# Memory softmax of a two-layer memory transformer: bias and sum inside the exponent

## The chip, the cores and the metric

The kernel runs on one core of one Trainium2 chip. The metric is device time in microseconds (us) of one execution, given as the median of several runs. The engines are named as the profile names them: PE is TensorE (matmuls and transpositions), PEld its weight loads, DVE is VectorE, ACT is ScalarE, POOL is GpSimd, and SP is SyncE, which issues DMAs.

## What is computed

Two layers, each of which is a recurrent attention with memory followed by a gated feed-forward network, are applied twice with the same weights. The sequence has 2048 tokens of 448 features. The attention goes through it in 64 segments of 32 tokens; each segment sees 8 memory rows and its own 32 tokens (40 keys), with 16 heads of 256 features, and leaves 8 new memory rows for the next segment.

```python
def _A_ref(x, mem0, Wq, Wk, Wv, Wo, seg_len):
    scale = Dh ** (-0.5)
    L = M + seg_len
    idx = jnp.arange(L)
    mask = (idx[:, None] < M) | (idx[:, None] >= idx[None, :])
    mem = mem0
    for s in range(n_seg):
        xs = x[:, s * seg_len:(s + 1) * seg_len, :].copy()
        h = jnp.concatenate([mem, xs], axis=1)
        q, k, v = (jnp.einsum('btd,dhe->bhte', h, W) for W in (Wq, Wk, Wv))
        scores = jnp.einsum('bhqe,bhke->bhqk', q, k) * scale
        scores = jnp.where(mask[None, None], scores, -1000000000.0)
        p = _softmax(scores, axis=-1)
        o = jnp.einsum('bhqk,bhke->bhqe', p, v)
        o = jnp.einsum('bhte,hed->btd', o, Wo)
        mem = o[:, :M, :].copy()
        outs.append(o[:, M:, :])

def _B_ref(x, W_gate, W_up, W_down):
    gate = x @ W_gate
    return (gate * (gate > 0) * (x @ W_up)) @ W_down

x = x + _A_ref(_layernorm(x), ...)
x = x + _B_ref(_layernorm(x), ...)
x = x + _A_ref(_layernorm(x), ...)
x = x + _B_ref(_layernorm(x), ...)
```

The three weights of the query and key side, and of the value and output side, can be multiplied together beforehand: with A = Wq Wk^T for each head, a score is h A h^T times the scale.

## The kernel before

**Stages.** A first stage (about the first 70 us) loads the weights, transposes them on PE and fuses them: `fuse_qk_parts` makes A (tiles `A_sb`, `A3`, `A3z`) and `fuse_vo` makes B = Wv Wo (`B_sb`). It goes through the 16 heads as 8 pairs p. Each pair's products stand in PSUM tiles `aps` and `mxw`, and `evac` moves them to SBUF: a plain copy on ACT (line 94) or on DVE (line 96).

**Steps.** Then `step(g, ff)` runs for g from 0 to 68. The attention of the first layer (chain 0) works on segment g, that of the second layer (chain 1) on segment g - 4; both chains share each step's instructions, with the keys of chain 0 and chain 1 side by side (2 x 40 columns). For g from 4 to 63 both chains are there; the four steps at either end have one. Odd steps also carry the feed-forward work of a block of two segments (`Feed`, argument `ff`); even steps do not.

**Order.** The order of all PE instructions is fixed by hand: `mm` and `tr` chain every matmul to the one before it (`in_order`). DVE, ACT and POOL each run their instructions in one queue, but a planner at build time chooses the order of that queue from when it expects each instruction to be ready; only instructions marked with `keep_in_program_order` are bound to the order of the code. PSUM tiles come from one pool of seven banks (tag `ps`) and one more bank.

**One step around the change.** Heads are worked in two halves, hf = 0 and 1. `open_banks` and `close_bank` make the projected queries (PSUM tile `prj`, 80 columns per matmul), which ACT or DVE casts into `TQ` and `TZ`. For half 1 the four banks are called c0, c2, c1, c3: c0, c2 and c3 are cast by ACT, c1 by DVE. Three kinds of scores are made: `scores_m(hf)` for the memory rows of both chains (PSUM tile `Sm`, 128 x 2 x 40: one partition for a head and a memory row of a chain, two blocks of 40 keys, of which the row needs only its own chain's), and `scores_x(hf)` for the token rows (`Sx`, 128 x 4 x 40). Each goes through a softmax: `weights_begin` (maximum, subtraction, exponent) and `weights_end` (sum, reciprocal, division). For the memory rows the reciprocal is multiplied by `blk`, a 128 x 2 tile of zeros and ones, which clears the block of the other chain. The results are `PM[hf]` and `PX[hf]`.

`flipped` (or `flipped_rows`) then transposes PM or PX on PE into PSUM (`pps`, `ppr`), and DVE copies it to `PT`. `weigh_m` or `weigh_m_rows` multiplies the keys `hk` with PT (PSUM tiles `ya`, `yb`, `ym`), `weigh_x` does so for the token rows (`y1`, `y2`, `y` in the profile), and copies on DVE and ACT (lines 94, 96, 661, 666) bring the results into the tiles Y and Z, which `project_out` and `project_tail` multiply with B (`ox`, `o`).

The order of PE in an even step with both chains, from the memory scores on: Sm of half 0; banks c0, c2, c1, c3 of half 1; the transposition of PM[0]; Sx of half 0; `ya` and `yb`; Sm and Sx of half 1; 69 matmuls of `project_out`; the transpositions of PM[1] and PX[0]; five more tiles of `project_out`; `ym` and `y`. In an odd step the feed's transposition stands ahead of Sm of half 1, and `project_out` of ten tiles and five rounds `gate_up` ahead of `ym`, with PM[1] and PX[0] transposed together (`ppr`) after three of these rounds.

Of the kernel before, what the change touches and what calls it, by code (L numbers as in the profile page):

```python
# [9 lines left out]
F32 = mybir.dt.float32  # L10
I32 = mybir.dt.int32
AF = mybir.ActivationFunctionType
ALU = mybir.AluOpType
AX = mybir.AxisListType
# [4 lines left out]
DH = 256  # L19
MEM = 8  # L20
SEG = 32
L = MEM + SEG
F = 1792
FT = 14
SCALE = DH ** -0.5
MASKVAL = -1.0e6
EPS = 1e-5
LAG = 4
BLK = 2
# [11 lines left out]
ROWS = (slice(0, 64), slice(64, 128))  # L41
# [12 lines left out]
def build_kernel(ctx, tc, A_x, A_mem0, A_Wq, A_Wk, A_Wv, A_Wo, B_W_gate, B_W_up, B_W_down, out,  # L54
                 ntiles=16, nseg=64):
    nc = tc.nc
    P = nc.NUM_PARTITIONS
# [23 lines left out]
    def mm(*a, **k):  # L81
        in_order(nc.tensor.matmul(*a, **k))  # L82
# [9 lines left out]
    def evac(eng, dst, src):  # L92
        if eng is nc.scalar:
            nc.scalar.copy(dst, src)  # L94
        else:
            eng.tensor_copy(dst, src)  # L96


    xa = [glob.tile([P, DM], BF, name=f"xa{i}") for i in range(3)]
    xp = [glob.tile([P, DM], BF, name=f"xp{i}") for i in range(2)]  # L100

    def block(i):
        return slice(TB * i, TB * i + TB)
# [11 lines left out]
                            op0=ALU.arith_shift_right, op1=ALU.bitwise_and)  # L115
    nc.vector.tensor_scalar(out=rowi[:, 2:3], in0=rowi[:, 0:1], scalar1=15, scalar2=None,
                            op0=ALU.bitwise_and)
# [9 lines left out]
    for b in range(4):  # L127
        o = 0 if b % 2 == 0 else MEM
        nc.vector.tensor_scalar(out=maskS[:, b, o:o + SEG], in0=keyf[:, b // 2, :], scalar1=rowf[:, 2:3],
                                scalar2=MASKVAL, op0=ALU.is_gt, op1=ALU.mult)  # L130

    blk = glob.tile([P, 2], F32, name="blk")
    nc.gpsimd.tensor_copy(blk[:, 1:2], rowf[:, 1:2])
    nc.gpsimd.tensor_scalar(out=blk[:, 0:1], in0=blk[:, 1:2], scalar1=-1.0, scalar2=1.0,
                            op0=ALU.mult, op1=ALU.add)
# [4 lines left out]
    A_sb = glob.tile([P, 3, 2, NT, 128], BF, name="A_sb")  # L140
    A3 = glob.tile([P, 2, 12, 128], BF, name="A3")
    A3z = glob.tile([P, 4, 128], BF, name="A3z")
# [71 lines left out]
    with tc.tile_pool(name="pre", bufs=3) as pre:  # L214
# [41 lines left out]
        def dims(t, r, e, c, n=1):  # L256
            o = 64 * c if r == 0 else DM + 64 * ((c + 1) % NPASS)
            return t[:, e, o:o + 64 * n]

        def halves(dst, lhs, rhs):  # L260
            for t in range(2):
                for eo in range(2):
                    mm(dst[ROWS[eo]], lhs(eo, 2 * eo + t), rhs(2 * eo + t), start=(t == 0), stop=(t == 1),
                       tile_position=(0, 64 * eo))

        def fuse_qk_parts(p, qk):
            hf, p4 = divmod(p, 4)
            mx_ps = psum.tile([P, 4, 128], F32, tag="ps", name="mxw")
            for n, (kd, eo) in enumerate([(kd, eo) for eo in range(2) for kd in range(3)] if p < 2 else
                                         [(kd, eo) for kd in range(3) for eo in range(2)]):  # L270
                if n == 3:
                    yield
                aps = psum.tile([P, 3, 128], F32, tag="ps", name="aps")
                for t in range(2):
                    e = 2 * eo + t
                    mm(aps[:, :, :], qk[:, e, kd * 128:kd * 128 + 128], dims(qk, 1, e, 0, 6),
                       start=(t == 0), stop=(t == 1))
                for t in range(2):
                    e = 2 * eo + t
                    mm(mx_ps[:, kd, eo * 64:eo * 64 + 64], qk[:, e, kd * 128:kd * 128 + 128], dims(qk, 1, e, 6),  # L280
                       start=(t == 0), stop=(t == 1))
                evac(nc.scalar if eo or kd == 2 else nc.vector,
                     A_sb[:, kd, hf, eo * 4 + p4:eo * 4 + p4 + 17:8, :], aps[:])
            aps = psum.tile([P, 3, 128], F32, tag="ps", name="aps")
            halves(aps, lambda eo, e: qk[:, e, 384:448], lambda e: dims(qk, 1, e, 0, 6))
            for eo in range(2):
                for t in range(2):
                    e = 2 * eo + t
                    mm(mx_ps[ROWS[hf], 3, eo * 64:eo * 64 + 64], qk[:, e, 384:448], dims(qk, 1, e, 6),
                       start=(t == 0), stop=(t == 1), tile_position=(0, 64 * hf))  # L290
            evac(nc.scalar, A3[:, hf, p4:p4 + 9:4, :], aps[:])
            evac(nc.vector, A_sb[:, 0:3, hf, 24 + p4, :], mx_ps[:, 0:3])
            evac(nc.scalar, A3z[ROWS[hf], p4, :], mx_ps[ROWS[hf], 3])

        def fuse_vo(p, vv, wo):
            hf, p4 = divmod(p, 4)
# [75 lines left out]
    main = ctx.enter_context(tc.tile_pool(name="main", bufs=1))  # L372
# [21 lines left out]
    TZ, PX, PM = [], [], []  # L394
# [97 lines left out]
    def moving(hb, j, idx, chains, rows=slice(0, P)):  # L492

        if len(chains) == 2:
            return hb[rows, j, idx * HI:(idx + 1) * HI].rearrange("p (c k) -> p c k", k=64)[:, :, 0:L]
        c = chains[0]
        return hb[rows, j, idx * HI + 64 * c:idx * HI + 64 * c + L]
# [61 lines left out]
    def queries(hf, g, kd):  # L559
        return TQ[hf][:, g, 2 * kd:2 * kd + 2, :] if kd < 3 else TZ[hf][:, g, :]  # L560

    def weights_of(*a):
        weights_end(*weights_begin(*a))

    def weights_begin(Sp, n, dst, keep, tag):

        mx = main.tile([P, n], F32, tag=f"mx{tag}", name="mx")
        nc.vector.tensor_reduce(mx[:], Sp[:], axis=AX.X, op=ALU.max)
        se = main.tile([P, n, L], F32, tag=f"se{tag}", name="se")
        nc.vector.tensor_tensor(se[:], Sp[:], mx[:].unsqueeze(2).to_broadcast([P, n, L]), op=ALU.subtract)  # L570
        nc.scalar.activation(se[:], se[:], AF.Exp, scale=SCALE)  # L571
        return se, n, dst, keep, tag

    def weights_end(se, n, dst, keep, tag):

        ssum = main.tile([P, n], F32, tag=f"ssum{tag}", name="ssum")
        nc.vector.tensor_reduce(ssum[:], se[:], axis=AX.X, op=ALU.add)  # L577
        rs = main.tile([P, n], F32, tag=f"rs{tag}", name="rs")
        nc.vector.reciprocal(rs[:], ssum[:])
        if keep is not None:  # L580
            nc.vector.tensor_tensor(rs[:], rs[:], keep, op=ALU.mult)
        nc.vector.tensor_tensor(dst[:, :, 0:L], se[:], rs[:].unsqueeze(2).to_broadcast([P, n, L]), op=ALU.mult)

    def flipped(src, n, tag):
# [25 lines left out]
    def step(g, ff):  # L610
# [21 lines left out]
        def scores_m(hf):  # L632
            if not ms:
                return
            Sp = psum.tile([P, 2, L], F32, tag="ps", name="Sm")
            for kd in range(4):
                mm(Sp[:, :, :], queries(hf, 2, kd), moving(hb, j, kd + kd // 3, (0, 1)), start=(kd == 0), stop=(kd == 3))
            weights_of(Sp, 2, PM[hf], blk[:], f"m{hf}")

        def scores_x(hf):  # L640
            Sp = psum.tile([P, 4, L], F32, tag="ps", name="Sx")
            if len(chains) == 1:
                mm(Sp[:, :, :], ident[:], maskS[:], start=True, stop=False, skip_group_check=True)
            for half in range(2):
                for c in chains:
                    for kd in range(4):
                        mm(Sp[:, 2 * half + c, :], queries(hf, 3 * c + half, kd), moving(hb, j, kd + kd // 3, (c,)),
                           start=(len(chains) == 2 and half == c == kd == 0),
                           stop=(half == 1 and c == chains[-1] and kd == 3), skip_group_check=True)
            return Sp  # L650

        def probs_x(hf, Sp):
            weights_of(Sp, 4, PX[hf], None, f"x{hf}")

        def weigh_m(hf, hk, PT):
            if not ms:
# [97 lines left out]
        def feed(*us):  # L754
            if ff is not None:
                for u in us:
                    ff.gate_up(u)
# [36 lines left out]
        if len(chains) == 2:  # L794
# [6 lines left out]
            Sx1 = scores_x(1)  # L801
            probs_x(0, Sx0)
        else:
# [4 lines left out]
            Sx1 = scores_x(1)  # L808
# [4 lines left out]
            load_some()  # L813
        if ff is not None:
            project_out(0, 0, 10)
            half1 = weights_begin(Sx1, 4, PX[1], None, "x1")
            feed(0, 1, 2)
            pt = flipped_rows([(PM[1], 1), (PX[0], 2)])
            feed(3, 4)
            weigh_m_rows(1, hk, pt)  # L820
            feed(5, 6)
            weigh_x(0, hk, pt[:, 128:384])
            weights_end(*half1)
            project_tail()
            ff.down()
            project_out(0, 10, NT)
            project_out(1, 0, 14)
            px1 = flipped(PX[1], 2, "x1")
            ff.norm2()
            project_out(1, 14, 24)  # L830
            ff.feed_on()
            ff.leave()
            project_out(1, 24, NT)
            finish()
            weigh_x(1, hk, px1)
            return
        project_out(0, 0, 23)
        probs_x(1, Sx1)
        pm = flipped(PM[1], 1, "m1")
        px0 = flipped(PX[0], 2, "x0")  # L840
# [88 lines left out]
```

## Time and profile before

| | |
|---|---|
| runs | 1578.43, 1579.52, 1586.14 us; median 1579.52 us |
| the profiled execution | 1585.95 us, its span from first to last instruction 1584.0 us |
| mean granted clock of TensorE | 0.990 |
| one pair of steps in the steady part (814.45 to 858.90 us) | 44.45 us: PE 44.45, PEld 41.55, DVE 32.10, ACT 22.37, POOL 4.56 us busy |
| DVE on the memory softmax (134 times; mean ns) | maximum 236, subtraction 235, sum 234, reciprocal 160, product with blk 157, division 232 |
| ACT on the memory softmax (134 times) | exponent 266 ns |

How to read it: the page's first part gives each engine's busy time, its share of the span and its number of instructions; the second part divides the span into 40 slices and gives the busy share of each in tenths. A line of the timeline has its start and duration in us, the engine, the line of the kernel, the operation, what it writes and reads, and how many instructions it stands for; in square brackets is how long the engine stood idle before it and what ended that. A line of the waits says which engine and line waited for which, with the total in us, how often, and the longest. In the table of groups by form the numbers are total busy us, mean ns of one, and the idle time ahead of them. Copies and casts are recorded on the line of their helper (94 and 96), so they are told apart by their tiles.

### The profile page before, as it was taken

How to read it: one execution, taken by the hardware profiler on the slowest of the kernel's cores; microseconds unless marked ns; L12 is line 12 of the kernel's file. 1: busy time of each engine (PE TensorE's matmuls, PEld its weight loads, DVE VectorE, ACT ScalarE, POOL GpSimd, SP SyncE). 2: the span in 40 equal slices, each digit the busy share in tenths (PEclk: the TensorE clock that was granted, in tenths of full speed). 3: DMA queues.
4: the chain of work that ended last, by engine and by line, in shares of the span. 5: the costliest groups of instructions: out<-in, count | busy, mean ns of one | idle time of the engine just before them, and what ended most of it. 6: DMA issues, size and time to landing. Idle time of an engine off the chain costs nothing.

```text
span 1584.0 us, 98180 instructions
## 1 busy us (share of the span) xinstructions
PE 1552.8 (98%) x45116; PEld 1426.0 (90%) x45116; DVE 1112.6 (70%) x3825; ACT 783.1 (49%) x2307; POOL 174.9 (11%) x308
## 2 busy tenths in 40 slices
PE   9889999999999999999999999999999999999997
PEld 7588899999999999999999999999999999999885
DVE  6755677776777777776777677777767777777663
ACT  6634445544455545554455545544445545544442
POOL 3201110111011111111011111011001111011110
PEclk9989999999999999999999999999999999999998
DMA  9530000000000000000000000000000000000000
GB/s 284 148 80 8 9 10 5 9 10 10 10 10 10 10 10 6 8 10 10 10 10 10 10 10 7 7 10 10 10 10 10 10 10 8 6 8 7 7 7 6
DMA packets 29469, 33.13 MB, mean 21 GB/s; under 512 B 3320, under 2 KB 28160, under 8 KB 29056
## 3 DMA queue, kind: packets, MB, share of 16 engines
q1 hardware_dynamic: 28848, 26.74, 6.2%
q8 instruction: 353, 5.78, 1.5%
q14 instruction: 60, 0.49, 0.1%
q10 hardware_dynamic: 144, 0.11, 0.1%
q0 software_dynamic: 64, 0.01, 0.0%
HBM read 23.18 MB, written 1.84 MB: 16 GB/s over the span
## 4 chain that ended last, share of the span: by engine, by line
PE 95%; DVE 2%; issue 1%; ACT 1%; DMA 1%; POOL 1%; SPq 0%; POOLq 0%; ACTq 0%; DVEq 0%
PE prj L82 30%; PE ox L82 25%; PE ups L82 10%; PE dps L82 6%; PE o L82 5%; PE y L82 4%; PE Sx L82 3%; PE Sm L82 2%; PE aps L82 1%; PE pps L85 1%; PE gps L82 1%; PE bps L82 1%; PE tps L85 1%; PE kps L85 1%; PE ym L82 1%
## 5 line engine op out<-in xcount | busy, mean ns | idle before, releaser
L82 PEld LDWEIGHTS <-B_sb 128*128 128x128 bf16 (+1 forms) x15456 | 495.1, 103 | 29.6 <-issue 21.6
L82 PE MATMUL prj<-hT,A_sb 128*128 128x80 bf16 (+1 forms) x11424 | 430.7, 200 | 0.1
L82 PEld LDWEIGHTS <-A_sb 128*128 128x128 bf16 x11424 | 406.3, 100 | 8.5 <-issue 0.2
L82 PE MATMUL ox<-Y,B_sb 128*128 128x80 bf16 (+4 forms) x5880 | 223.1, 199 | 1.9 <-DVE Y L661 1.9
L94 ACT CAST TQ<-prj 128x480 bf16<-128x480 f32 (+1 forms) x380 | 183.1, 494 | 83.7 <-PE prj L82 59.2
L82 PE MATMUL ox<-Z,B_sb 128*128 128x80 bf16 (+2 forms) x5712 | 217.6, 199 | 1.3 <-DVE Z L661 1.3
L82 PE MATMUL ups<-xT,Wgu_sb 64*128 64x128 bf16 (+1 forms) x3332 | 191.3, 214 | 1.3 <-DVE hh L458 0.8
L82 PE MATMUL gps<-xT,Wgu_sb 64*128 64x128 bf16 (+1 forms) x3332 | 191.3, 214 | 0.4 <-ACT xT L444 0.3
L82 PEld LDWEIGHTS <-Wgu_sb 64*128 64x128 bf16 x6664 | 179.7, 95 | 4.4 <-issue 2.3
L96 DVE CAST TQ<-prj 128x480 bf16<-128x480 f32 (+1 forms) x228 | 129.5, 574 | 17.3 <-PE prj L82 11.7
L458 DVE SCALAR_TENSOR_TENSOR hh<-gps,ut 128x256 bf16<-128x256 f32 (+1 forms) x238 | 94.5, 407 | 48.2 <-ACT ut L457 35.4
L457 ACT CAST ut<-ups 128x256 bf16<-128x256 f32 (+1 forms) x238 | 85.5, 359 | 82.7 <-PE gps L82 64.1
L94 ACT CAST Y<-y 64x128 bf16<-64x128 f32 (+2 forms) x256 | 89.4, 379 | 46.5 <-DVE Y L96 41.5
L96 DVE CAST Y<-y 64x128 bf16<-64x128 f32 (+2 forms) x256 | 102.2, 420 | 14.2 <-ACT Y L94 4.3
L94 ACT COPY hT<-tps 128x256 bf16<-128x256 bf16 x32 | 11.9, 372 | 199.0 <-DVE hT L96 199.0
L96 DVE CAST Z<-y 64x128 bf16<-64x128 f32 (+2 forms) x256 | 99.2, 418 | 12.4 <-ACT Z L94 5.5
L589 DVE COPY PT<-pps 128x128 bf16<-128x128 bf16 (+1 forms) x206 | 49.9, 256 | 80.5 <-PE pps L85 77.7
L94 ACT CAST Z<-y 64x128 bf16<-64x128 f32 (+2 forms) x256 | 89.2, 378 | 23.8 <-DVE Z L96 17.4
L82 PE MATMUL dps<-Wd_sb,hh 128*128 128x448 bf16 x476 | 99.3, 362 | 0.0
L94 ACT CAST TZ<-prj 64x320 bf16<-64x320 f32 (+2 forms) x152 | 56.1, 380 | 86.4 <-DVE TZ L96 78.5
L577 DVE TENSOR_REDUCE ssum<-se 128x2 f32<-128x80 f32 (+1 forms) x270 | 70.8, 274 | 35.8 <-ACT se L571 33.6
L82 PE MATMUL prj<-hT,A 64*128 64x80 bf16 (+1 forms) x3264 | 93.9, 196 | 1.8 <-issue 1.4
(130 smaller groups left out, 2265.7 us busy)
## 6 DMA issues: line engine op xcount, KB each, us to landing
wo<-in_A_Wo_dram SPq DMA_DIRECT2D x8, 448.0 KB, 5.1
nat<-in_A_Wq_dram SPq DMA_DIRECT2D x8, 384.0 KB, 6.1
nat<-in_A_Wk_dram SPq DMA_DIRECT2D x8, 384.0 KB, 6.2
nat<-in_A_Wv_dram SPq DMA_DIRECT2D x8, 384.0 KB, 6.1
xa<-in_A_x_dram SPq DMA_DIRECT2D x32, 56.0 KB, 2.3
xa<-xp SPq DMA_DIRECT2D x32, 56.0 KB, 1.9
out_dram<-xa SPq DMA_DIRECT2D x32, 56.0 KB, 2.0
xp<-in_A_x_dram SPq DMA_DIRECT2D x30, 56.0 KB, 2.1
```

Source lines behind the costliest of these rows:

```text
L82: in_order(nc.tensor.matmul(*a, **k))
L85: in_order(nc.tensor.transpose(*a))
L94: nc.scalar.copy(dst, src)
L96: eng.tensor_copy(dst, src)
L457: nc.scalar.copy(ut[:, :, n], ups[:, :, n])
L458: nc.vector.scalar_tensor_tensor(out=hh[:, 2 * u:2 * u + 2, n], in0=gps[:, :, n], scalar=0.0, in1=ut[:, :, n], op0=ALU.max, op1=ALU.mult)
L577: nc.vector.tensor_reduce(ssum[:], se[:], axis=AX.X, op=ALU.add)
L589: nc.vector.tensor_copy(PT[:], pps[:].rearrange("p b q -> p (b q)"))
```

## The change

The memory rows get a softmax of their own, `weights_two`. The maximum is returned with its sign turned and serves as the bias of the exponent, which so reads the scores from PSUM itself; each of the two blocks of 40 keys has its own exponent, because each block has its own maximum, and each exponent also returns the sum of its block. The division and the mask by `blk` are one operation for each block, with two scalar columns. As a bias is added after the exponent's scale, the scale 1/16 moves into the weights A: `scaled` takes the place of `evac` in `fuse_qk_parts`, and the mask value is multiplied by the same scale. The softmax of the token rows keeps its form, without the scale and without the mask argument.

```diff
-MASKVAL = -1.0e6
+MASKVAL = -1.0e6 * DH ** -0.5
...
+    def scaled(eng, dst, src):
+        if eng is nc.scalar:
+            nc.scalar.activation(dst, src, AF.Copy, scale=SCALE)
+        else:
+            eng.tensor_scalar(out=dst, in0=src, scalar1=SCALE, scalar2=None, op0=ALU.mult)
...
-                evac(nc.scalar if eo or kd == 2 else nc.vector,
-                     A_sb[:, kd, hf, eo * 4 + p4:eo * 4 + p4 + 17:8, :], aps[:])
+                scaled(nc.scalar if eo or kd == 2 else nc.vector,
+                       A_sb[:, kd, hf, eo * 4 + p4:eo * 4 + p4 + 17:8, :], aps[:])
...
-            evac(nc.scalar, A3[:, hf, p4:p4 + 9:4, :], aps[:])
-            evac(nc.vector, A_sb[:, 0:3, hf, 24 + p4, :], mx_ps[:, 0:3])
-            evac(nc.scalar, A3z[ROWS[hf], p4, :], mx_ps[ROWS[hf], 3])
+            scaled(nc.scalar, A3[:, hf, p4:p4 + 9:4, :], aps[:])
+            scaled(nc.vector, A_sb[:, 0:3, hf, 24 + p4, :], mx_ps[:, 0:3])
+            scaled(nc.scalar, A3z[ROWS[hf], p4, :], mx_ps[ROWS[hf], 3])
...
-    def weights_begin(Sp, n, dst, keep, tag):
+    def weights_two(Sp, dst, tag):
+
+        mx = main.tile([P, 2], F32, tag=f"mx{tag}", name="mx")
+        nc.vector.tensor_reduce(mx[:], Sp[:], axis=AX.X, op=ALU.max, negate=True)
+        se = main.tile([P, 2, L], F32, tag=f"se{tag}", name="se")
+        ssum = main.tile([P, 2], F32, tag=f"ssum{tag}", name="ssum")
+        for c in range(2):
+            nc.scalar.activation(se[:, c, :], Sp[:, c, :], AF.Exp, bias=mx[:, c:c + 1], accum_out=ssum[:, c:c + 1])
+        rs = main.tile([P, 2], F32, tag=f"rs{tag}", name="rs")
+        nc.vector.reciprocal(rs[:], ssum[:])
+        for c in range(2):
+            nc.vector.tensor_scalar(out=dst[:, c, 0:L], in0=se[:, c, :], scalar1=rs[:, c:c + 1], scalar2=blk[:, c:c + 1],
+                                    op0=ALU.mult, op1=ALU.mult)
+
+    def weights_begin(Sp, n, dst, tag):
...
-        nc.scalar.activation(se[:], se[:], AF.Exp, scale=SCALE)
-        return se, n, dst, keep, tag
+        nc.scalar.activation(se[:], se[:], AF.Exp)
+        return se, n, dst, tag
...
-        if keep is not None:
-            nc.vector.tensor_tensor(rs[:], rs[:], keep, op=ALU.mult)
...
-            weights_of(Sp, 2, PM[hf], blk[:], f"m{hf}")
+            weights_two(Sp, PM[hf], f"m{hf}")
...
-            weights_of(Sp, 4, PX[hf], None, f"x{hf}")
+            weights_of(Sp, 4, PX[hf], f"x{hf}")
...
-            half1 = weights_begin(Sx1, 4, PX[1], None, "x1")
+            half1 = weights_begin(Sx1, 4, PX[1], "x1")
```

More of the change, by code (lines that the diff above doesn't have):

```diff
@@ L570, in weights_begin, with weights_end @@
         nc.vector.tensor_tensor(se[:], Sp[:], mx[:].unsqueeze(2).to_broadcast([P, n, L]), op=ALU.subtract)
-        nc.scalar.activation(se[:], se[:], AF.Exp, scale=SCALE)
-        return se, n, dst, keep, tag
-    def weights_end(se, n, dst, keep, tag):
+        nc.scalar.activation(se[:], se[:], AF.Exp)
+        return se, n, dst, tag
+    def weights_end(se, n, dst, tag):
         ssum = main.tile([P, n], F32, tag=f"ssum{tag}", name="ssum")
```

## The prediction

> **What bounds the kernel now.** I read the page's busy shares and slices first, then TensorE's own waits, then the timeline of one steady pair of steps.
>
> ```profile
> PE 1552.8 (98%) x45116; PEld 1426.0 (90%) x45116; DVE 1112.6 (70%) x3825; ACT 783.1 (49%) x2307; POOL 174.9 (11%) x308
> ...
> PE   9889999999999999999999999999999999999997
> ...
> PEclk9989999999999999999999999999999999999998
> ```
>
> TensorE is busy for 1552.8 of 1584.0 us at full clock. The stretches from 192.40 to 236.90 us and from 814.45 to 858.90 us are each one pair of steps, and TensorE is busy in all 44.50 and 44.45 us of them, VectorE in 32.1 and ScalarE in 22.4. What frees VectorE or ScalarE in the steady part can give time back only where TensorE waits for them. These are its waits that end behind a softmax:
>
> ```profile
> PE ya L82 <- DVE PT L589: 2.7, 7, 0.5
> ...
> PE ox L82 <- DVE Y L661: 1.9, 4, 0.5
> ...
> PE ox L82 <- DVE Z L661: 1.3, 3, 0.5
> ...
> PE ppr L85 <- DVE PX L582: 0.9, 1, 0.9
> ...
> PE pps L85 <- DVE PM L582: 0.5, 1, 0.5
> ```
>
> The numbers after the colon are us in total, times and the longest; the totals add up to 7.3 us, none of it in the steady pairs. So the change can win a few us at most, and the question is whether it makes TensorE wait where it now just does not. TensorE's order is fixed by hand, so a late tile delays all behind it. Here is a memory softmax of the first half in an even step (start, us, engine, line):
>
> ```profile
> 819.77 0.24 DVE L568 TENSOR_REDUCE mx<-Sm 128x2 f32<-128x80 f32 x1 [0.22 <-PE Sm L82]
> 819.96 0.27 ACT L628 COPY hk<-kps 128x128 bf16<-128x128 bf16 x1
> 820.04 0.24 DVE L570 TENSOR_TENSOR se<-Sm,mx 128x80 f32<-128x80 f32 x1
> 820.32 0.27 ACT L571 ACTIVATE se<-se 128x80 f32<-128x80 f32 x1
> 820.49 1.12 ACT L94 CAST TQ<-prj 128x480 bf16<-128x480 f32 x2
> 820.62 0.24 DVE L577 TENSOR_REDUCE ssum<-se 128x2 f32<-128x80 f32 x1 [0.34 <-ACT se L571]
> 820.89 0.17 DVE L579 RECIPROCAL rs<-ssum 128x2 f32<-128x2 f32 x1
> 821.09 0.16 DVE L581 TENSOR_TENSOR rs<-rs,blk 128x2 f32<-128x2 f32 x1
> 821.28 0.24 DVE L582 TENSOR_TENSOR PM<-se,rs 128x80 bf16<-128x80 f32 x1
> 821.70 0.66 DVE L96 CAST TQ<-prj 128x480 bf16<-128x480 f32 x1 [0.17 <-PE prj L82]
> ...
> 822.14 0.22 PE L85 MATMUL pps<-ident,PM 128*128 128x128 bf16 x1
> ...
> 822.40 0.23 DVE L589 COPY PT<-pps 128x128 bf16<-128x128 bf16 x1
> ...
> 822.68 0.22 PE L82 MATMUL ya<-PT,hk 128*128 128x128 bf16 x1
> ```
>
> The reader is to see three things. PM is ready at 821.52, 0.6 us before its transposition: that looks like slack. But VectorE then has the TQ cast of bank c1 (821.70 to 822.36), and the PT copy starts at 822.40, released by that cast's end and by the transposition's end (822.36) at once; ya starts 0.05 us after the copy. So if the softmax holds VectorE beyond 821.70, cast, copy and ya move by as much and TensorE waits. The real slack is the 0.18 us from 821.52 to 821.70. The odd step has the same shape: PM ends at 839.64, the cast starts at 839.76 (0.12 us), the PT copy at 840.46, ya at 840.74.
>
> **The change, part by part.** Per memory softmax (134, two in each of 67 steps) it takes away the subtraction (235 ns mean), the sum (234), the product with blk (157) and the division (232): 858 ns of VectorE. It adds two TENSOR_SCALARs of 128x40 with two scalar columns each, one more exponent, and reading out two sums. The rows that price these:
>
> ```profile
> L571 ACT ACTIVATE se<-se 128x80 f32<-128x80 f32 x134 | 35.6, 266 | 6.3 <-DVE se L570 0.2
> ...
> L187 DVE TENSOR_SCALAR xn<-xp,mv,rstd 128x64 bf16<-128x64 bf16 x33 | 9.7, 294 | 0.0
> ...
> L94 ACT CAST TQ<-prj 128x48 bf16<-128x48 f32 x40 | 8.0, 199 | 10.9 <-PE prj L82 10.3
> ```
>
> *Two divisions.* The nearest row with two scalar columns is xn at 128x64, 294 ns; behind its longer neighbour it starts some 0.09 us early (a pair of 0.39 and 0.30 took 0.60). Low: four maskS operations of 128x32 took 0.68 us, so two are 0.40 with the last one's end. High: two of 0.294 without overlap, 0.59. I take 0.53. VectorE still saves about 0.3 us each time, 134 x 0.3 = 40 us, all under a busy TensorE: worth nothing in the steady part by itself.
>
> *Two exponents and their sums.* The rows at 160 and 80 columns (329 and 266 ns) give 0.79 ns a column, so 234 ns at 40 columns. Neither a bias column on ScalarE nor a sum returned by it is in the trace. Low: both are free and the second starts 0.1 us before the first ends (as the TQ casts at 820.49 do behind the exponent), 0.37 us in all. High: a serial instruction for each sum as dear as the 128x48 cast (0.20), and 0.11 for a bias column (what both columns together make of xn's 294 ns against the 180 of a 128x32 sum of two tensors on line 741), so 2 x (0.234 + 0.11 + 0.20) = 1.09. I take half of the 0.11 for the one column, and the sum as an instruction of its own at 199 - 48 x 0.79 = 0.16 and 0.03 to start it: 2 x (0.234 + 0.055 + 0.19) = 0.95 us. That is nearer to the high end, because every ScalarE row of this trace has a fixed part of 0.16 to 0.20, and a total can be read only behind the last element.
>
> In the Trainium skill, "ScalarE: Activation LUTs", section "What ACT_TABLE_LOAD costs", says that each per-partition pointer operand adds about 93 ns to an activation, and that the fixed part is paid per instruction: it speaks against splitting one exponent in two. By it the block would be 0.95 + 2 x 0.038 = 1.03 us, and the sum below 60 x 0.08 = 5 us more; no run here shows it yet.
>
> *The path, even step.* Maximum ready at 820.01 as now. ScalarE is free behind the hk copy (0.27, less 0.1 overlap) at about 820.14. Exponents and sums to 821.09; 0.03 to VectorE; reciprocal 0.16; 0.03; divisions 0.53: 821.84, where PM ends at 821.52 today. An operation that waits for nothing starts up to 0.09 before the one ahead ends; with 0.06 of that, the cast of c1 starts at 821.78 instead of 821.70: 0.08 us late. Odd step: the hk copy starts at 838.07, so 838.24 + 0.95 + 0.75 - 0.06 = 839.88 for a cast now at 839.76: 0.12 late. Mean 0.10 us over the 60 steps with two chains: 6 us. By the low ends (0.37 and 0.40) the cast isn't touched: 0, and no gain, as the transposition's end still releases the PT copy. By the high ones (1.09, 0.59, no overlap) it is 0.44 to 0.49 late: 60 x 0.46 = 28 us.
>
> Queued behind the exponents on ScalarE are the TQ casts of c0 and c2: 820.49 becomes about 821.1, their end at 821.6 about 822.2, still before c3's cast at 822.35, where ScalarE idles 0.73 us now. That idle time covers the 0.6 us; without it Sm of the second half (822.96, c3's cast ends 822.91) would wait as long.
>
> *The second half, even step.* PM is now ready at 825.86 and PX at 825.28; their transpositions start at 825.99 and 826.04. VectorE is busy without a hole from 822.80. The exponents would hold ScalarE from 823.64 to 824.6, where the Sx exponent starts at 823.87 today; its sum, reciprocal and division (0.31, 0.17, 0.32) then come behind the two divisions of PM on VectorE. Counted on: reciprocal to 824.8, PM to 825.3, sum 825.6, reciprocal 825.8, PX 826.1, against 825.98 wanted: 0.13 us late, with bounds of 0 (VectorE has 0.3 us less to do) and 0.3. Times 30: 4 us. In the odd step three gate and up rounds stand between, and the transpositions are at 845.25 with PM and PX ready at 844.35 and near 844.6: 0.6 us of cover, no cost.
>
> *The weights' scale* (lines 282 to 293): casts become scaled casts, six on ScalarE and three on VectorE for each of eight pairs of heads. An activation of 160 columns at 329 ns against a cast's 480 ns at 384 columns says some 0.03 us more each: 8 x 6 x 0.03 = 1.4 us of ScalarE between 10 and 45 us, where it is 80% busy and TensorE all of 20 to 40; hidden, 0 to 1 us. The one table load, at 1.18 us, serves copies and exponents alike already. MASKVAL's new value costs nothing.
>
> Sum: 6 + 4 = 10 us on the profiled execution's 1585.95 us. The three shown runs have a median of 1579.52 (1578.43 to 1586.14), so the profiled one lies at their top; on the median it is **1589.5 us**.
>
> **The rivals.** (a) *Not slower*: if the sum comes with the exponent almost free, the block is 0.4 to 0.85 us, the divisions end before 821.70, and nothing on TensorE moves: 1579.5. For it: VectorE loses work; against it: the fixed part in every ScalarE row. (b) *Faster*: the 7.3 us of TensorE's waits above go, 1572. Against it: most of them are behind the PT and Y copies, which stay. (c) *Another order on VectorE*: instructions run there in the order in which they were thought ready, not in the code's (at 822.80 the maximum of Sx runs before that of Sm, 823.37, though the code has it after). If c1's cast is put ahead of reciprocal or divisions, PM ends near 822.9, its transposition comes 0.84 us late: 60 x 0.84 = 50 us, 1630. It decides from a block of about 1.25 us on, as planned. (d) *It doesn't do what it says*: a table load for each change between scaled copy and exponent; the copies and exponents that already alternate show none. 1% or less, counted with (c).
>
> **How the numbers follow.** About 0.5%, 8 us, is what a measurement of this kernel can tell from no change. Forecast of a late cast 0.49, (a) 0.36, (b) 0.05, (c) 0.10. Of the forecast's chance 0.02 ends within 8 us. So slower 0.57, same 0.38, faster 0.05. The range goes from 1575 (part of the waits won) to 1622 (the high ends: 28 us, 30 x 0.3 = 9, and a few for the scaled casts and the ramps); beyond are (b) and (c). The forecast alone: 1584 to 1615.
>
> **What would show it.** In the changed trace: the start of c1's cast against the maximum's end (1.69 us now); a wait of ya on PT in the steady pairs, 0 now; the length from the first exponent to the reciprocal (0.98 forecast, the way to VectorE with it); the pair of steps longer than 44.45 us; busy VectorE down by 30 to 45 us. I'm wrong if the pair stays at 44.45, or if PM's transposition rather than ya is what waits.

## The result, and the profile after

The changed kernel takes 1594.65 us (median of 5 runs, 1594.02 to 1596.57), the kernel before 1580.76 us beside it (5 runs, 1578.43 to 1586.84): a ratio of 1.0079 with a 95% interval of 1.0058 to 1.0100. It is slower by 13.9 us. The forecast was 1589.5 us, slower, by a softmax that is late in two places. It is slower, by a softmax that is late, but in a third place, and in neither of those two; that the number is near is luck.

The page of the changed kernel, first part, and TensorE's waits that end behind VectorE's work on a softmax or feed (us in total, times, longest), with the line of the kernel before for the first of them below:

```profile
PE 1556.3 (98%) x45116; PEld 1427.8 (90%) x45116; DVE 1084.8 (68%) x3557; ACT 820.2 (51%) x2709; POOL 175.7 (11%) x308
```

```profile
PE ups L82 <- DVE hh L464: 8.1, 29, 0.4
...
PE ya L82 <- DVE PT L607: 2.4, 7, 0.4
...
PE ox L82 <- DVE Y L679: 1.8, 4, 0.5
...
PE ox L82 <- DVE Z L679: 1.3, 3, 0.5
...
PE ppr L85 <- DVE PX L600: 0.7, 1, 0.7
```

```profile
PE ups L82 <- DVE hh L458: 0.8, 2, 0.6
```

VectorE lost 27.8 us of work and ScalarE gained 37.1, as the change says. One wait is new in the steady part, and it comes 29 times (2 before): `ups`, a matmul of the feed, waits for `hh`, VectorE's product of an earlier round. The wait of ya on PT, which the prediction looked for, is 2.4 us in 7 times, where it was 2.7 in 7 before. A pair of steps, taken from one Sm of the first half in an even step to the next such Sm, in the two kernels (columns: us, then busy us and instructions of PE, PEld, DVE, ACT, POOL, then the clock, DMA share and GB/s):

```profile
819.41:863.87 44.46, 44.46 (x1299) 41.56 (x1296) 32.11 (x111) 22.38 (x66) 4.58 (x8) 1.00 0.04 9
```

```profile
822.71:867.65 44.94, 44.66 (x1300) 41.65 (x1296) 31.28 (x103) 23.46 (x78) 4.60 (x8) 1.00 0.03 9
```

The pair is 0.48 us longer and the clock is the same; 29 or 30 such pairs are 14 us, the whole of the loss. Of the two halves of a pair, the one that begins in the even step has 18.06 us in both kernels, the one that begins in the odd step has 26.40 before and 26.88 after. The loss is made in the odd steps, which are the ones that carry a feed.

**The place that the prediction named.** VectorE and ScalarE of the changed kernel in the first half of an even step:

```profile
823.07 0.24 DVE L574 TENSOR_REDUCE mx<-Sm 128x2 f32<-128x80 f32 x1 [0.22 <-PE Sm L82]
824.12 0.17 DVE L580 RECIPROCAL rs<-ssum 128x2 f32<-128x2 f32 x1 [0.81 <-ACT se L578]
824.33 0.52 DVE L582 TENSOR_SCALAR PM<-se,rs,blk 128x40 bf16<-128x40 f32 x2
825.00 0.66 DVE L96 CAST TQ<-prj 128x480 bf16<-128x480 f32 x1 [0.16 <-PE prj L82]
825.70 0.23 DVE L607 COPY PT<-pps 128x128 bf16<-128x128 bf16 x1
```

```profile
823.42 0.30 ACT L578 ACTIVATE se<-Sm,mx 128x40 f32<-128x40 f32 x1
823.61 0.20 ACT L578 ACTIVATION_READ_ACCUMULATOR se<-Sm,mx 128x1 f32 x1
823.70 0.29 ACT L578 ACTIVATE se<-Sm,mx 128x40 f32<-128x40 f32 x1
823.88 0.21 ACT L578 ACTIVATION_READ_ACCUMULATOR se<-Sm,mx 128x1 f32 x1
823.97 1.03 ACT L94 CAST TQ<-prj 128x480 bf16<-128x480 f32 x2
```

The sum is an instruction of its own, as taken. But the four overlap: each starts 0.09 to 0.19 us after the one ahead, and all four take 0.67 us, not 0.95. PM is ready at 824.85, 1.54 us after the maximum (before 1.51), and c1's cast starts at 825.00, 1.69 us after it, exactly as before, still released by TensorE.

**The place where it is lost.** VectorE in an odd step, from the last subtraction on, in the kernel before, with ScalarE and TensorE below:

```profile
842.63 0.32 DVE L570 TENSOR_TENSOR se<-Sx,mx 128x160 f32<-128x160 f32 x1
843.17 0.55 DVE L577 TENSOR_REDUCE ssum<-se 128x2 f32<-128x80 f32 x2 [0.22 <-ACT se L571]
843.63 0.16 DVE L579 RECIPROCAL rs<-ssum 128x2 f32<-128x2 f32 x1
843.70 0.30 DVE L577 TENSOR_REDUCE ssum<-se 128x4 f32<-128x160 f32 x1
843.92 0.15 DVE L581 TENSOR_TENSOR rs<-rs,blk 128x2 f32<-128x2 f32 x1
843.99 0.23 DVE L579 RECIPROCAL rs<-ssum 128x4 f32<-128x4 f32 x2
844.14 0.21 DVE L582 TENSOR_TENSOR PM<-se,rs 128x80 bf16<-128x80 f32 x1
844.27 0.55 DVE L582 TENSOR_TENSOR PX<-se,rs 128x160 bf16<-128x160 f32 x2
844.74 0.76 DVE L458 SCALAR_TENSOR_TENSOR hh<-gps,ut 128x256 bf16<-128x256 f32 x2
```

```profile
841.87 0.97 ACT L444 COPY xT<-tps 64x384 bf16<-64x384 bf16 x2 [0.40 <-DVE xT L442]
842.87 0.72 ACT L571 ACTIVATE se<-se 128x80 f32<-128x80 f32 x3
```

```profile
845.28 0.22 PE L85 MATMUL ppr<-ident,PX 64*128 64x64 bf16 x4
845.34 0.22 PE L82 MATMUL ups<-xT,Wgu_sb 64*128 64x128 bf16 x1
```

and the same in the changed kernel:

```profile
845.78 0.33 DVE L590 TENSOR_TENSOR se<-Sx,mx 128x160 f32<-128x160 f32 x1
846.86 0.17 DVE L580 RECIPROCAL rs<-ssum 128x2 f32<-128x2 f32 x1 [0.76 <-ACT se L578]
847.07 0.52 DVE L582 TENSOR_SCALAR PM<-se,rs,blk 128x40 bf16<-128x40 f32 x2
847.49 0.54 DVE L597 TENSOR_REDUCE ssum<-se 128x4 f32<-128x160 f32 x2
847.95 0.30 DVE L599 RECIPROCAL rs<-ssum 128x4 f32<-128x4 f32 x2
848.16 0.55 DVE L600 TENSOR_TENSOR PX<-se,rs 128x160 bf16<-128x160 f32 x2
848.63 0.75 DVE L464 SCALAR_TENSOR_TENSOR hh<-gps,ut 128x256 bf16<-128x256 f32 x2
```

```profile
845.17 0.97 ACT L450 COPY xT<-tps 64x384 bf16<-64x384 bf16 x2 [0.38 <-DVE xT L448]
846.17 0.29 ACT L578 ACTIVATE se<-Sm,mx 128x40 f32<-128x40 f32 x1
...
846.63 0.20 ACT L578 ACTIVATION_READ_ACCUMULATOR se<-Sm,mx 128x1 f32 x1
```

```profile
848.60 0.22 PE L85 MATMUL ppr<-ident,PX 64*128 64x64 bf16 x4
849.10 0.21 PE L82 MATMUL ups<-xT,Wgu_sb 64*128 64x128 bf16 x1 [0.28 <-DVE hh L464]
```

VectorE now stands idle for 0.76 us (before 0.22) until ScalarE has the second sum, because the exponents of Sm stand on ScalarE behind two copies of xT that end at 846.14, and are 0.66 us long where one exponent took 0.27. Behind the wait come all the reciprocals and divisions, PX of the second half among them, and only then the first hh. From Sm of the second half (841.18 before, 844.50 in the changed kernel) to the first hh it is 3.56 us before and 4.13 now. Of the 0.57 us between them 0.37 lie ahead of VectorE's first operation behind the wait (1.99 us behind Sm in the kernel before, 2.36 in the changed one). The other 0.20 lie behind it: from there to hh VectorE took 1.57 us before and takes 1.77 now, with nine operations in place of ten.

The transposition `ppr` is on time. The next matmul, the fourth round's, starts 0.05 us after the first hh ends, and 0.44 us later than before (4.60 us after Sm for 4.16). The profile's 0.28 us of waiting is less than that. A round takes two PSUM banks, `gps` and `ups`, and the pool has seven. When `ppr` takes its two, ScalarE has read `ups` of the first two rounds (its copies end at 847.57 and 848.35). So `gps` of three rounds, one `ups` and the two banks of `ppr` are held, six of seven, and the fourth round needs two: it waits for the bank that hh of the first round reads. This count is worked out from the kernel and these times, as the profile names hh and not the bank; the run that moves the transposition tests it.

### The profile page after: what moved, and what is told of

Same layout as the page of the kernel before. It is cut to its first block, busy times and chain, and to the rows that moved or that the text cites. A ratio compares the mean times of both kernels' runs of the same rounds, so it can differ in the third digit from the quotient of the medians.

```text
span 1593.1 us, 98346 instructions
## 1 busy us (share of the span) xinstructions
PE 1556.3 (98%) x45116; PEld 1427.8 (90%) x45116; DVE 1084.8 (68%) x3557; ACT 820.2 (51%) x2709; POOL 175.7 (11%) x308
## 4 chain that ended last, share of the span: by engine, by line
PE 85%; DVE 7%; ACT 3%; issue 2%; POOL 1%; DMA 1%; SPq 0%; POOLq 0%; ACTq 0%
PE prj L82 29%; PE ox L82 23%; PE dps L82 6%; PE o L82 5%; PE ups L82 5%; PE y L82 4%; PE gps L82 2%; PE Sx L82 2%; PE Sm L82 1%; ACT xT L450 1%; PE aps L82 1%; ACT se L578 1%; DVE PM L582 1%; PE pps L85 1%; PE bps L82 1%
## 5 line engine op out<-in xcount | busy, mean ns | idle before, releaser
L94 ACT CAST TQ<-prj 128x480 bf16<-128x480 f32 (+1 forms) x380 | 178.4, 504 | 73.2 <-PE prj L82 52.4
L82 PE MATMUL dps<-Wd_sb,hh 128*128 128x448 bf16 x476 | 96.0, 353 | 0.0
L183 POOL TENSOR_SCALAR rstd<-mv 128x1 f32<-128x1 f32 x67 | 15.3, 229 | 727.0 <-DVE mv L181 726.9
```

The source lines that it names most:

```text
L183: nc.gpsimd.tensor_scalar(out=rstd[:], in0=mv[:, 1:2], scalar1=EPS, scalar2=None, op0=ALU.add)
```

## The experiments

Theory T: the loss is made in the odd steps alone, where the second half's memory softmax makes the first hh late and the fourth round waits for its bank. Rivals: every new softmax costs about 0.1 us wherever it stands (S); the scaled weights cost (W); the prediction's own places. `weights_old` is the memory softmax of before without the exponent's scale, which stays in the weights in all kernels but the one control that is made from the kernel before.

**The scale alone**, all memory softmaxes old:

```diff
-            weights_two(Sp, PM[hf], f"m{hf}")
+            (weights_two if False else weights_old)(Sp, PM[hf], f"m{hf}")
```

> The scale stays folded into the weights, and every memory softmax has its old form (subtraction, one exponent, sum, product with blk, division). Theory T (the loss of 13.9 us is made in the odd steps alone: the second half's memory softmax ends late on VectorE, the first feed product hh behind it is late, and the fourth gate/up round waits for a PSUM bank): 1581 us, within 2 us of before, the pair of steps back at 44.45 us. Rival W (the scaled casts of the first stage cost, the first memory scores start 1.2 us later in the changed kernel than before): 1582 to 1583. Rival S (each of the 134 memory softmaxes costs its 0.1 us wherever it stands): 1581.

Measured: 1580.97 us against 1579.89 before, ratio 1.0002 (0.9991 to 1.0012). The scaled casts cost nothing that can be measured; W falls.

**The new softmax everywhere but in the second half of feed steps:**

```diff
-            weights_two(Sp, PM[hf], f"m{hf}")
+            (weights_two if hf == 0 or ff is None else weights_old)(Sp, PM[hf], f"m{hf}")
```

> The new softmax everywhere but in the second half of steps that carry a feed, which has the old one: 101 of 134 are new. T: 1581 us, the pair of steps at 44.45. S: 101/134 of 13.9, that is 1591. The prediction's own place (first half, c1's cast; second half of even steps): all of the loss stays, 1594.

Measured: 1579.78 us, ratio 0.9998 (0.9988 to 1.0007). 101 new softmaxes, the prediction's two places among them, cost nothing that can be measured (the odd part has 26.42 us for 26.40). S falls, and so do these places.

**Only there:**

```diff
-            weights_two(Sp, PM[hf], f"m{hf}")
+            (weights_two if hf == 1 and ff is not None else weights_old)(Sp, PM[hf], f"m{hf}")
```

> The new softmax only in the second half of steps that carry a feed, 33 of 134, the old one elsewhere. T: all of the loss, 1593 to 1595, the pair at 44.92. S: 33/134 of it, 1584. The prediction's own place: none of it, 1581.

Measured: 1594.84 us, ratio 1.0094 (1.0073 to 1.0114): all of the loss, from 33 softmaxes. The new wait is in its trace:

```profile
PE ups L82 <- DVE hh L464: 8.5, 29, 0.3
```

**The banks: the transposition a round later.** All softmaxes are new, one line is moved:

```diff
-            feed(0, 1, 2)
+            feed(0, 1, 2, 3)
             pt = flipped_rows([(PM[1], 1), (PX[0], 2)])
-            feed(3, 4)
+            feed(4)
```

> The changed kernel with one line moved: the transposition of PM and PX in feed steps, with its two PSUM banks, stands behind the fourth gate/up round instead of the third. All softmaxes stay new. T says that the fourth round waits because three rounds and the two banks of the transposition fill all seven, so without the latter it starts at once and the bank of the first round is wanted a round (0.78 us) later: the wait of 0.47 us is gone, 1581 us. If TensorE really waits for PM or for the exponents themselves, the 0.47 us stay or turn up at the moved transposition: 1590 or more. A rival within T: the later PT copies hold back ym and y, which costs up to 0.3 us each, 1590.

Measured: 1583.66 us, ratio 1.0020 (1.0009 to 1.0032). The fourth round follows the third at once (the transposition behind it starts 4.85 us after Sm for 4.07, one round of 0.78 later), and some 10 of the 14 us are gone; the softmax itself was not touched. The time lies between the two that were named, nearer to 1581. From Sm to Sm the odd part has 26.53 us, 0.13 more than before, of which 0.08 stand ahead of ym.

**Its control, the same move in the kernel before:**

> The kernel before with the same one line moved as in the run that set the transposition of PM and PX a round later, as its control; nothing of the change is in it. That run kept 0.13 us a pair (26.53 for 26.40 from Sm to Sm). If the 0.13 is what the later PT copies cost, it is here too: pair 44.58, 1583 us. If it is a rest of the softmax's lateness, this one is at 44.45 and 1580.

Measured: the odd part is at 26.40 us, as without the move, so the 0.13 above are a rest of the softmax's lateness (the PT copy is behind the late hh on VectorE). The time, though, is 1584.53 against 1581.83 us, ratio 1.0019 (1.0007 to 1.0032), and the profiled execution is the fastest of its ten runs (1580.96 us), so the trace does not show where the 2.7 us are. They are not in the steady pairs, and both moves together, below, do not have them. The granted clock may have a part: its mean is 0.9904 in these ten runs and 0.9916 in the sixteen of the kernel before. Among those sixteen, 0.001 less goes with some 0.9 us more, so 1 us of the 2.7 is an estimate for it. The rest stays open.

**Two more operations on ScalarE** ahead of the exponents, in the second half of feed steps:

```diff
+        for _ in range(dose):
+            nc.scalar.activation(idle_t[:], Sp[:], AF.Copy)
         for c in range(2):
             nc.scalar.activation(se[:, c, :], Sp[:, c, :], AF.Exp, bias=mx[:, c:c + 1], accum_out=ssum[:, c:c + 1])
...
-            weights_two(Sp, PM[hf], f"m{hf}")
+            weights_two(Sp, PM[hf], f"m{hf}", 2 if hf == 1 and ff is not None else 0)
```

> The changed kernel with two idle copies of Sm (128x80, PSUM to SBUF) put on ScalarE ahead of the exponents, in the second half of feed steps alone; what they write is not used. T: the exponents, the reciprocal on VectorE and the first hh come later by what the two take in the queue, some 0.13 us each (0.22 less 0.09 overlap), and so the wait: 30 x 0.26 = 8 us more, 1602 us. If the wait hangs on VectorE's work alone, or if the exponents have slack, 1595.

Measured: 1597.60 us, ratio 1.0102 (1.0084 to 1.0119), 0.04 us a pair instead of 0.26: a miss of the size. In its trace the first exponent of Sx stands between the two copies, and its sum, reciprocal and division stand ahead of PM's on VectorE: the planner gave another order, so little of the dose reached hh. The first hh starts 0.04 us later, and so does the fourth round. So this run doesn't test what it was made for, beyond that the round still follows hh.

**Without the sums.** The read-outs are left out, and the reciprocal is that of the first exponent:

```diff
-            nc.scalar.activation(se[:, c, :], Sp[:, c, :], AF.Exp, bias=mx[:, c:c + 1], accum_out=ssum[:, c:c + 1])
+            nc.scalar.activation(se[:, c, :], Sp[:, c, :], AF.Exp, bias=mx[:, c:c + 1])
...
-        nc.vector.reciprocal(rs[:], ssum[:])
+        nc.vector.reciprocal(rs[:], se[:, :, 0])
```

> The changed kernel in which the exponents return no sum: it is left out in all memory softmaxes, and the reciprocal is taken of the first exponent of each block, so the outputs differ. The two read-outs (0.20 us each, 0.09 each in the queue) are gone from ScalarE. T: the reciprocal comes some 0.2 us earlier, the wait falls from 0.47 to 0.27 us: 1588 to 1590 us. If the read-outs cost nothing where they stand: 1595.

Measured: 1591.57 us, ratio 1.0060 (1.0043 to 1.0076). The pair is 0.18 us shorter than in the changed kernel: the two read-outs cost 0.09 us each, what they take in ScalarE's queue, not their 0.20. The time is a little above the 1588 to 1590 that was named.

**Another order on VectorE.** All softmaxes new, TensorE's order untouched; sum, reciprocal and division of PX of the second half, which is transposed some 11 us later, stand behind the last hh:

```diff
-            weights_end(*half1)
+            with tc.issue_after(ff.hh_ins.ins):
+                weights_end(*half1)
```

(`hh_ins` is the latest product on line 464, here that of the last round.)

> The changed kernel, with an order given on VectorE: sum, reciprocal and division of PX of the second half in feed steps (0.27 + 0.13 + 0.25 us in the queue), which nothing needs for 10 us, stand behind the last hh instead of ahead of the first. TensorE's order and all softmaxes stay as changed. T: the first hh starts 0.6 us earlier, its bank is free before the fourth round, no wait: pair 44.45, 1580 to 1582 us. If TensorE waits for anything else of the softmax than VectorE's queue ahead of hh, part of the 14 us stays: 1585 or more.

Measured: 1586.88 us, ratio 1.0030 (1.0016 to 1.0044). VectorE in an odd step of this kernel (Sm of the second half at 794.48):

```profile
797.04 0.52 DVE L582 TENSOR_SCALAR PM<-se,rs,blk 128x40 bf16<-128x40 f32 x2
797.47 0.32 DVE L597 TENSOR_REDUCE ssum<-se 128x4 f32<-128x160 f32 x1
797.82 0.18 DVE L599 RECIPROCAL rs<-ssum 128x4 f32<-128x4 f32 x1
798.03 0.33 DVE L600 TENSOR_TENSOR PX<-se,rs 128x160 bf16<-128x160 f32 x1
798.27 0.75 DVE L464 SCALAR_TENSOR_TENSOR hh<-gps,ut 128x256 bf16<-128x256 f32 x2
```

One sum, reciprocal and division of PX are left ahead of hh. It starts 0.33 us earlier, not 0.6. Each of the three starts 0.03 us behind the end of the one that it needs, so one set takes 0.80 us up to hh, where the two sets of the changed kernel, which fill each other's gaps, took 1.14 (847.49 to 848.63). So 0.14 us a pair stay. With this the runs make a row (us after Sm of the second half, medians of the 29 steady odd steps of each trace):

| kernel | first hh starts | fourth round starts | difference |
|---|---|---|---|
| before | 3.56 | 4.16 | 0.60 |
| PX behind hh | 3.80 | 4.27 | 0.47 |
| without the sums | 3.95 | 4.42 | 0.47 |
| changed | 4.13 | 4.60 | 0.47 |
| two more on ScalarE | 4.17 | 4.64 | 0.47 |

Wherever the round is late it follows the start of hh by 0.47 us, hh's own 0.42 and 0.05. Before the change it didn't wait, with 0.13 us to spare.

**Both moves together:**

> The changed kernel with both moves: the transposition of PM and PX behind the fourth gate/up round, and the sum, reciprocal and division of PX of the second half behind the last hh. Each alone left 0.13 to 0.14 us a pair. T: hh has both its start 0.33 us earlier and its bank wanted 0.78 us later, so nothing is left: pair 44.45, within 2 us of before (1578 to 1582), though all 134 softmaxes are new; no gain either, since TensorE has nothing to wait for in the kernel before. If the new softmax has a cost of its own elsewhere: 1583 to 1586.

Measured: 1580.85 us against 1579.93, ratio 1.0005 (0.9994 to 1.0016). The odd part has 26.42 us. All 134 softmaxes are new and the loss is gone; there is no gain, as the kernel before has nothing for TensorE to wait for. No version here beats the kernel before.

**Is the prediction's place a limit at all?** In the kernel that is new all but in the second half of feed steps, two idle operations between exponents and divisions in each first half:

```diff
+        for _ in range(dose):
+            nc.vector.tensor_tensor(se[:], se[:], se[:], op=ALU.max)
         rs = main.tile([P, 2], F32, tag=f"rs{tag}", name="rs")
...
-            weights_two(Sp, PM[hf], f"m{hf}")
+            if hf == 0:
+                weights_two(Sp, PM[hf], f"m{hf}", 2)
+            else:
+                (weights_two if ff is None else weights_old)(Sp, PM[hf], f"m{hf}")
```

> New softmax in all but the second half of feed steps (which run was as fast as before), and in the first half of every step two idle operations on VectorE (the maximum of se with itself, 128x80, in place) between exponents and divisions, some 0.40 us more of VectorE. Their only aim is to see whether the place that the prediction named is a limit: there, PM ends 0.10 to 0.15 us before c1's cast. If the cast, the PT copy and ya follow without slack, the cast is 0.2 to 0.3 us late, ya too, in 60 steps: 12 to 18 us more, 1592 to 1598, and TensorE's waits name PT of line 623 ahead of ya. If there is more slack behind the cast than read from the trace: 1580 to 1584.

Measured: 1585.53 us, ratio 1.0036 (1.0021 to 1.0052), 5.6 us more, above one of the ranges that were named and well below the other. An odd step of it (maximum of Sm from 789.95 to 790.19):

```profile
791.73 0.52 DVE L584 TENSOR_SCALAR PM<-se,rs,blk 128x40 bf16<-128x40 f32 x2
792.16 0.65 DVE L96 CAST TQ<-prj 128x480 bf16<-128x480 f32 x1
792.73 0.22 DVE L623 COPY PT<-pps 128x128 bf16<-128x128 bf16 x1
```

The cast starts 1.97 us after the maximum's end, 0.27 late, ya starts 0.13 late, 0.05 us behind the PT copy, and the pair is 0.13 us longer: 3.9 us in 30 pairs; where the rest of the 5.6 is isn't shown. In the even step the cast is 0.11 late and costs nothing. The list of TensorE's waits does not name PT more often than before (2.3 us, 7 times), so that sign did not come. The place is a limit, but some 0.14 us further off than the trace was read: the PT copy started 0.04 us behind the cast's end before, and it starts 0.08 us ahead of it here (the cast ends at 792.81). The change didn't reach it.

## Why the prediction was right, and where it was wrong

**The bound** held: TensorE decides, and nothing saved on VectorE was won. The change frees 27.8 us of VectorE (40 counted) and none of it shows.

**The price of the parts.** These are the rows of the new instructions:

```profile
L578 ACT ACTIVATE se<-Sm,mx 128x40 f32<-128x40 f32 x268 | 76.9, 294 | 10.1 <-DVE mx L574 9.1
L582 DVE TENSOR_SCALAR PM<-se,rs,blk 128x40 bf16<-128x40 f32 x268 | 68.9, 304 | 3.5
L578 ACT ACTIVATION_READ_ACCUMULATOR se<-Sm,mx 128x1 f32 x268 | 54.0, 201 | 0.0
```

The divisions are 0.52 us for a pair (0.53 taken). The exponent is 294 ns (0.289 taken), and the read-out 201 ns (0.19). The 294 came out near by two errors that nearly cancel. The 234 ns without a bias column were taken from rows that read SBUF, and this exponent reads PSUM. The idle copies of the run with two more operations on ScalarE read PSUM without a bias column and have 234 ns at 128x80, where the exponent from SBUF had 266; by 0.79 ns a column that is some 0.20 us at 40 columns. So, as an estimate, PSUM saves 0.03 us and the bias column costs 0.09, not 0.055. The error that counts is in the sum of the block: exponents and read-outs were added end to end on the ground that a total is read behind the last element, while the queue starts each 0.1 us early. 0.67 us came of 0.95. The Trainium skill, "ScalarE: Activation LUTs", section "What ACT_TABLE_LOAD costs", says that back-to-back activations overlap by some 93 ns; the trace has 0.11 to 0.12, and it holds for the read-outs as well. Its 93 ns for a pointer operand, which the bias column is, agree with the 0.09. The 5 us more that the prediction worked out by them did not come: it put them on rows from SBUF, and at a place that cost nothing.

**The first half** (6 us, by c1's cast): 0. Two terms were off. With 0.67 for 0.95 the divisions end 0.15 us before the cast. And "cast, copy and ya move by as much" has some 0.14 us of slack behind the cast, as the two idle operations showed: even the late casts that were forecast (0.08 and 0.12 us) would have cost next to nothing. That run also showed that the chain described is real. **The second half of even steps** (4 us): 0. PM ends 2.34 us after Sm (828.60), as counted. But PX was counted behind both divisions of PM, 0.13 us late, and VectorE takes its sum ahead of them (827.85 for 828.09): PX ends at 829.12, 0.22 us before its transposition at 829.34, which starts as long after Sm as before.

**The odd step** is the step that failed. "0.6 us of cover, no cost" followed PM and PX to their transposition, which is still on time, and stopped there. It did not ask what else stands on VectorE behind the softmax (the hh of the feed), nor which PSUM bank that work holds. This cost the 14 us. The forecast's 10 us were for the other two places, so its nearness is luck and no merit of the working.

**The signs that it named.** Two came: the pair is longer than 44.45 us (44.94), and VectorE has less to do, though by 27.8 us and not by 30 to 45. The others did not: c1's cast starts 1.69 us after the maximum as before, ya does not wait for PT in the steady pairs, and from the first exponent to the reciprocal it is 0.70 us (823.42 to 824.12) and not 0.98.

**The weights' scale** (0 to 1 us): 1.0002 with an interval of 0.9991 to 1.0012. **The rivals**: faster, another order for c1's cast, and table loads did not happen. "Not slower" holds for each part but one.

## What to carry to other kernels

When an engine off the critical path gets a longer wait, follow all that is queued behind it, not only the tile that the change makes: here the late one was a product of another stage, and its price was a PSUM bank. A trace with no wait at all says nothing of how near the next wait is; count the banks that the fixed order holds at once and read the gap (0.13 us here) from release to need. A bubble that comes back in one size can point to such a resource: the Trainium skill says in "Trainium Kernel Development and Optimization", section "Best Practices", that consistent bubbles can mean that SBUF or PSUM ran out. This trace agrees, with the same wait of 0.28 us 29 times, for a round that is 0.44 us late.

## What the runs showed of the hardware

An exponent that returns its sum leaves two rows, the activation (294 ns at 128x40) and a read-out (201 ns). The activation is as long without a sum (295 ns in the run without the sums). The read-out lengthens ScalarE's queue by only 0.09 us, and VectorE can use the sum 0.03 us after it ends (824.09 to 824.12). An operation on VectorE that needs the one ahead starts 0.03 us behind its end (797.79 to 797.82), one that doesn't need it starts up to 0.09 us before (hh at 798.27, the division ends at 798.36). So a chain of three took 0.80 us alone, where two such chains that fill each other's gaps took 1.14, which is where half of the gain from the other order went.
